# A planned attention and channel-mix kernel: first loads by pair, heads mended in the difference, more work free to go to VectorE, a new order

## The chip, the cores and the metric

One core of one Trainium2 chip runs the whole program. The engines are TensorE (PE, with its weight loads as PEld), VectorE (DVE), ScalarE (ACT), GpSimd (POOL) and SyncE (SP), which here issues every transfer. The metric is the device time of one execution in microseconds; the median of several runs is given, and one execution is taken by the hardware profiler.

## The reference

Blockwise causal attention over q, k and v, each 8 x 8 heads x 576 x 64 in float32, and then an RWKV channel mix on its result (8 x 576 x 512). Cut to what matters:

```python
scores = np.matmul(q, k.transpose(0, 1, 3, 2)) / np.sqrt(D)
mask = (pos[:, None] // 64) >= (pos[None, :] // 64)
attn = softmax(np.where(mask, scores, -1e9))
x = np.matmul(attn, v)                # then heads side by side: b, s, 512
x_prev = x one position earlier       # zeros at the head of each batch
xk = mu_k * x + (1 - mu_k) * x_prev
xr = mu_r * x + (1 - mu_r) * x_prev
k = np.maximum(xk @ w_k, 0)           # 512 -> 1024
out = sigmoid(xr @ w_r) * (k * k @ w_v)
```

## The kernel before

Attention goes by batch (b, 0 to 7), and in a batch by pairs of heads (pr, 0 to 3); a group g is two pairs, and Q is the half of the heads that values are formed for. The channel mix goes by chunks c of positions over all batches: two of 256 positions and eight of 512. Batches are 576 long, so seven batch heads lie inside a chunk.

Every piece of work is a task of a planner (`Plan`) with an engine, a cost, dependencies and the buffers that it takes from rings. TensorE's order is a list written out by name (`TENSOR`). For tasks that more than one engine can do (`flex`), a table (`WHERE`) names the engine. The other engines' queues, and SP's queue of transfers, are laid out by `Plan.order`: tasks are sorted by due time, which is worked back from TensorE's order, and taken when the plan holds them ready. All this runs when the program is built; on the chip each engine works through its own queue in order, with semaphores between them.

Names in TensorE's order, with the profile's lines:

- `q{b}{pr}{n}` (L470): turns the queries (n = 0) or keys (n = 1) of a pair for batches 0 and 1, nine matmuls against an identity. Before it, two loads into `t_ld` (L373) of 288 KB each, one per x, and two casts into `t_nl` (`qk{b}{g}{n}{x}`) must be done, and a copy `ev` out of PSUM follows. One load holds one head of each of the group's two pairs: pair 0 in partitions 0 to 63, pair 1 in 64 to 127.
- For batches 2 to 7 there is no such product: loads, casts into `NB` (L392, L398), a copy of the tail on GpSimd (L516), and then a transposing DMA on SP's queue, `turn` (L534), one for each pair, 24 in all, into `t_qkt`.
- `s{b}{pr}{i}` (L652, L660): scores of a pair, three pieces i, and `s{b}t{Q}` for the last 64 keys. Each piece is followed by an exponential on ScalarE (L679) and, where a piece has a diagonal block, by setting its masked quarter to zero on GpSimd (`zero`, L688).
- `d{b}{Q}`, `e0{Q}` (L725): sums of the exponentials; reciprocal and spreading on VectorE follow (L777, L786). `v{b}{Q}{i}` (L725): values, then their scaling into `t_xt` on VectorE (L833, L835).
- For each chunk and each quarter cc of the 512 channels, `add_mix` forms the difference `t_d` of neighbouring positions (L907, on GpSimd or VectorE), and from it `t_xk` and `t_xr` on VectorE (L920). In a chunk with a batch head inside, GpSimd then writes that column of `t_xk` and `t_xr` anew (`fix`, L935), after the last quarter.
- `k{c}{jc}` (L958): four matmuls of `xk @ w_k`; a relu on ScalarE (L969), and a square (`sq`, L976, L978) on any of three engines. `r{c}{jt}` (L993) and tanh (L1004). `p{c}{jt}` (L1024): eight matmuls of `k*k @ w_v`, the last product on VectorE (L1036), and the store (L1042).
- Until the first `k` task the planner puts idle TensorE time to filling products against the identity (L1062).

Of the kernel before, what the change touches and what calls it, by code (L numbers as in the profile page):

```python
# [24 lines left out]
q000 q001 q011 q010 s000 s010 q031 s001 s011 q020 q021 q030 d00 v000 s012 s030  # L25
q100 q110 s002 s020 s0t0 s021 s032 d01 q101 v010 s0t1 e00 s031 v001 v002 s022
s100 q111 s101 k00 k02 k01 s110 q120 s111 e01 v011 v012 q131 s112 s1t0 q130
k03 s102 q121 k13 k15 k07 k05 k14 k11 k16 d10 s120 s122 k12 k17 r01 k10 s121
v100 v102 v101 s130 s131 r00 r10 r11 s1t1 s132 k04 k06 s200 d11 v111 v110 s201
p11 s202 p00 s210 s212 p01 s2t0 p10 v112 k20 s211 k22 r22 r23 k25 r20 k24 k21  # L30
d20 s230 s231 k26 k27 s232 r21 k23 v200 v201 s2t1 s220 s222 v202 s221 p20 s300
s301 d21 v211 v210 s302 v212 p23 p22 p21 k30 k31 k34 r32 s310 s311 r31 k36 k35
s3t0 s312 r30 k37 s320 s321 d30 k32 k33 s322 s330 v301 v300 v302 s331 s332 r33
s3t1 p31 d31 s400 s402 p33 v312 v311 v310 p30 p32 s401 k40 k41 k42 k43 k47
s410 s411 k46 r40 k45 r43 s4t0 s412 k44 r42 s430 s431 r41 d40 v400 v402 s432
s420 p41 s421 s422 p40 s4t1 v401 d41 s500 s501 p43 v411 v410 s5t0 s510 v412
s512 s502 p42 s511 s530 k50 k51 k57 s532 s520 k56 d50 r53 k53 r50 k52 k55 s531
s5t1 v500 v502 v501 s522 s521 r52 k54 s600 r51 d51 v511 v510 s601 s602 v512
p50 s610 s6t0 p51 p53 s620 s611 p52 s630 s612 k60 k63 s621 s632 k62 k66 k65
r62 k67 s631 k61 d60 s6t1 s622 k64 r60 v600 v602 v601 p60 r63 d61 s700 s702  # L40
p63 r61 v612 v611 v610 s710 s730 p62 s7t0 s731 p61 s712 s7t1 r71 r72 s701 s720
k70 k72 k74 s711 s721 k71 k73 k76 d70 s732 s722 k75 v700 v701 r70 d71 r73 k77
v711 v702 v710 p73 p70 p72 p71 v712 k80 k81 k82 k83 k86 k85 k84 k87 r81 r82
r83 r80 p83 p81 p82 p80 r92 r91 k90 k93 k96 k92 k91 k95 k94 k97 r90 r93 p91
p90 p92 p93b p93a
# [31 lines left out]

class Plan:

    LAT = {"PE": 0.26, "ACT": 0.19, "DVE": 0.16, "POOL": 0.16, "SP": 1.9}
    SWITCH = 0.095
    AHEAD = 25.0
    DMA = 2.0
    BLOCK, FIRST, FETCH = 256, 183, 5.0

    def __init__(self, rings):
# [191 lines left out]
def kernel(  # L281
# [12 lines left out]
    nc = tc.nc  # L294
# [840 lines left out]
```

## Time and profile before

| what | value |
|---|---|
| median of 5 runs | 270.44 us (269.43 to 271.48) |
| the profiled execution | 269.09 us |
| its span | 267.3 us, granted clock 0.994 |
| first product | at 6.86 us |
| DMA, whole span | 51.51 MB, 193 GB/s mean |
| zero blocks on GpSimd (L688) | 128, 208 ns mean |
| relu on ScalarE (L969), 512 columns | 64, 612 ns mean |
| mends on GpSimd (L935) | 7 of `t_xk`, 277 ns mean; 7 of `t_xr`, 409 ns mean |
| turning transfers (L534) | 24, on SP's queue 1.26 to 3.82 us, median 2.10 |

The span runs from the first instruction to the last; what lies between it and the execution's time is before and after it. Busy time of an engine is the union of its instructions; two instructions that follow each other overlap at their ends, so the mean of one times its count is a little more than the busy time. A line such as "A <- B: us, times, longest" says that A's engine stood idle until B ended. The DMA share is the mean of 16 DMA engines, and it can pass 1.0 where packets overlap. A piece of the chain of work is a start, a duration and what ran.

### The profile page before, as it was taken

What the parts mean: (1) busy time and instruction counts of PE and PEld (TensorE: products, weight loads), DVE (VectorE), ACT (ScalarE), POOL (GpSimd) and SP (SyncE); (2) the same over time, 40 slices, a digit from 0 to 9 for tenths busy, and PEclk for the clock granted to TensorE, in tenths of its full rate; (3) what the DMA queues carried; (4) which work ended last, traced back from release to release, by engine and by line L of the source; (5) the groups of instructions that cost most, each with busy time, mean ns of one, the idle gap of its engine ahead of it and who ended that gap; (6) DMA issues with size and microseconds to landing.
All of it is one profiled execution on the core that took longest, in us unless ns stands there. A gap on an engine that the chain in (4) does not pass through costs nothing.

```text
span 267.3 us, 9966 instructions
## 1 busy us (share of the span) xinstructions
PE 248.4 (93%) x4112; PEld 130.3 (49%) x4112; DVE 203.3 (76%) x474; ACT 195.5 (73%) x310; POOL 123.1 (46%) x271
## 2 busy tenths in 40 slices
PE   0999979999999999999989899899999999999995
PEld 0676566554445435544445345444554455444443
DVE  2378998889259976999598988987899099895323
ACT  2699998995999179829966899759758971490750
POOL 3664588537365254633345446354603563270020
PEclk9997999999999999999999999999999999999999
DMA  7999999999989999989979999999995100302104
GB/s 227 317 224 255 255 317 293 275 264 206 223 205 224 201 205 320 184 200 278 207 181 187 183 206 303 172 199 229 296 197 152 42 5 30 129 0 105 55 1 157
DMA packets 118301, 51.51 MB, mean 193 GB/s; under 512 B 102768, under 2 KB 109168, under 8 KB 118256
## 3 DMA queue, kind: packets, MB, share of 16 engines
q1 hardware_dynamic: 118256, 50.88, 82.4%
q8 instruction: 32, 0.52, 0.8%
q14 instruction: 13, 0.11, 0.2%
HBM read 33.56 MB, written 9.44 MB: 161 GB/s over the span
## 4 chain that ended last, share of the span: by engine, by line
PE 56%; ACT 14%; DMA 12%; DVE 7%; issue 5%; SPq 2%; POOL 2%; POOLq 0%; ACTq 0%
PE t_mm L1024 19%; PE t_mm L958 13%; PE t_mm L993 7%; PE t_mm L725 7%; ACT t_e L679 7%; DMA t_ld<-in_q_dram 5%; PE t_s L652 5%; DMA t_qkt<-NB 5%; ACT t_kr L969 3%; SPq L373 2%; DMA t_ld<-in_k_dram 2%; PE t_mm L470 2%; PE t_s L660 2%; ACT NB L392 1%; DVE t_xr L920 1%
## 5 line engine op out<-in xcount | busy, mean ns | idle before, releaser
L679 ACT ACTIVATE t_e<-t_s 128x1024 f16<-128x1024 f32 x96 | 96.1, 1033 | 14.5 <-PE t_s L660 7.4
L958 PE MATMUL t_mm<-t_xk,WK 128*128 128x512 f16 (+1 forms) x320 | 68.7, 358 | 0.8 <-POOL t_xk L935 0.5
L1024 PE MATMUL t_mm<-WV,t_k 128*128 128x512 f16 (+1 forms) x296 | 66.3, 374 | 0.3 <-DVE t_xt L833 0.3
L969 ACT ACTIVATE t_kr<-t_mm 128x512 f32<-128x512 f32 (+1 forms) x80 | 43.0, 569 | 20.5 <-PE t_mm L958 19.3
L688 POOL MEMSET t_e<- 64x128 f16 x128 | 24.4, 208 | 61.8 <-ACT t_e L679 60.0
L958 PEld LDWEIGHTS <-WK 128*128 128x128 f16 x320 | 29.7, 98 | 31.4 <-issue 2.4
L1024 PEld LDWEIGHTS <-t_k 128*128 128x128 f16 x296 | 27.2, 98 | 31.9 <-issue 2.1
L652 PE MATMUL t_s<-t_qkt 64*128 64x256 bf16 (+3 forms) x272 | 35.2, 327 | 3.8 <-ACT t_e L679 2.1
L993 PE MATMUL t_mm<-WR,t_xr 128*128 128x512 f16 x144 | 35.6, 380 | 0.4 <-DVE t_o L1036 0.4
L978 POOL TENSOR_TENSOR t_k<-t_kr 128x512 f16<-128x512 f32 (+1 forms) x26 | 24.0, 931 | 25.7 <-ACT t_kr L969 25.5
L833 DVE TENSOR_TENSOR t_xt<-t_mm,t_rd 128x448 f32<-128x448 f32 (+6 forms) x56 | 30.6, 596 | 6.2 <-PE t_mm L725 5.8
L907 POOL TENSOR_TENSOR t_d<-t_xt 128x512 f32<-128x512 f32 (+1 forms) x24 | 25.5, 1070 | 13.3 <-DVE t_xt L833 12.7
L920 DVE SCALAR_TENSOR_TENSOR t_xr<-t_d,MUR,t_xt 128x512 f16<-128x512 f32 (+1 forms) x40 | 31.5, 811 | 0.0
L1036 DVE SCALAR_TENSOR_TENSOR t_o<-t_t,t_mm 128x512 f32<-128x512 f32 (+1 forms) x37 | 24.0, 664 | 9.3 <-PE t_mm L1024 8.8
L920 DVE SCALAR_TENSOR_TENSOR t_xk<-t_d,MUK,t_xt 128x512 f16<-128x512 f32 (+1 forms) x40 | 29.0, 748 | 1.7 <-POOL t_d L907 1.7
L1004 ACT ACTIVATE t_t<-t_mm 128x512 f32<-128x512 f32 x36 | 21.5, 611 | 11.4 <-PE t_mm L993 11.2
L725 PE MATMUL t_mm<-t_e,VO 128*32 128x64 f16 (+4 forms) x1056 | 27.7, 248 | 1.0 <-issue 1.0
L978 DVE TENSOR_TENSOR t_k<-t_kr 128x512 f16<-128x512 f32 (+1 forms) x29 | 20.1, 710 | 11.0 <-ACT t_kr L969 11.0
L777 DVE RECIPROCAL t_c<-t_mm 128x128 f32<-128x128 f32 (+1 forms) x18 | 15.5, 864 | 16.9 <-PE t_mm L725 16.9
L660 PE MATMUL t_s<-t_qkt 64*128 64x64 bf16 x320 | 23.9, 195 | 1.7 <-ACT t_e L679 1.5
L725 PEld LDWEIGHTS <-VO 128*32 128x32 f16 x1184 | 19.0, 97 | 10.8 <-issue 6.3
L993 PEld LDWEIGHTS <-t_xr 128*128 128x128 f16 x144 | 13.1, 98 | 16.2 <-issue 1.8
(60 smaller groups left out, 270.5 us busy)
## 6 DMA issues: line engine op xcount, KB each, us to landing
out_dram<-t_o SPq DMA_DIRECT2D x35, 256.0 KB, 3.5
t_vl<-in_v_dram SPq DMA_DIRECT2D x32, 256.0 KB, 5.4
t_ld<-in_k_dram SPq DMA_DIRECT2D x48, 128.0 KB, 3.9
t_ld<-in_q_dram SPq DMA_DIRECT2D x24, 256.0 KB, 4.2
t_ld<-in_q_dram SPq DMA_DIRECT2D x8, 288.0 KB, 5.4
t_ld<-in_k_dram SPq DMA_DIRECT2D x8, 288.0 KB, 5.2
t_ld<-in_moe_w_k_dram SPq DMA_DIRECT2D x8, 256.0 KB, 5.5
t_ld<-in_moe_w_v_dram SPq DMA_DIRECT2D x8, 256.0 KB, 4.1
```

Of the source, the lines that this page charges most:

```text
L652: nc.tensor.matmul(PS[:, h, col:col + J * w].rearrange("p (j n) -> p j n", j=J), keys, ask[:, 0:CUT].rearrange("d (p j) -> d j p" if b < T ...
L660: nc.tensor.matmul(PS[:, h, col:col + D], keys, ask[:, CUT:S], start=True, stop=True)
L679: nc.scalar.activation(tiles["e", b, pr][:, :, i, :], tiles["ps", b, pr, i], AF.Exp, scale=ISQ)
L725: nc.tensor.matmul(ps[g * R:g * R + R], lhs, e, start=start, stop=stop, tile_position=(0, g * R))
L833: nc.vector.tensor_tensor(x[:, 0], num[:, 0], r, ALU.mult)
L907: (nc.vector if eng == "DVE" else nc.gpsimd).tensor_tensor(tiles["d", c, cc][:, 0:w], x[:, cc, o + 1:o + w + 1], x[:, cc, o:o + w], ALU.su ...
L920: nc.vector.scalar_tensor_tensor(tiles[name, h][:, cc, o:o + w], tiles["d", c, cc][:, 0:w], (MUK1, MUR1)[n][:, cc:cc + 1], xt_tile(c)[:, c ...
L958: nc.tensor.matmul(ps[:, 0:w], WK[:, cc, jc * P:(jc + 1) * P], tiles["xk", h][:, cc, o:o + w], start=(cc == 0), stop=(cc == CCn - 1))
L969: nc.scalar.activation(tiles["kr", c, jc][:, 0:w], tiles["pk", c, jc][:, 0:w], AF.Relu)
L978: (nc.vector if eng == "DVE" else nc.gpsimd).tensor_tensor(K2, KR, KR, ALU.mult)
L993: nc.tensor.matmul(ps, tiles["xr", h][:, cc, o + jt * P:o + (jt + 1) * P], WR[:, cc], start=(cc == 0), stop=(cc == CCn - 1))
L1024: nc.tensor.matmul(ps[:, 0:w], tiles["k2", h][:, jc, off:off + P], WV[:, jc, cols], start=(jc == 0), stop=(jc == JCn - 1))
```

## The change

Five things change.

1. For the first group of batch 0, each of the four loads is split by pair: eight loads of 64 partitions (144 KB) and eight casts, and a product of pair y waits only for the casts that hold y. All other groups are as before.
2. The batch heads are mended in the difference: after a quarter's `t_d` is formed, one column is copied from `t_xt` over it, on the engine that formed it, so that `t_xk` and `t_xr` come out right by themselves. The two `fix` operations per batch head go; four copies of one column per head come.
3. Zero blocks and relus become `flex`, open to GpSimd or VectorE, and to ScalarE or VectorE. The exponential is written for the used columns alone; all pieces use 512, so its shape stays.
4. The planner's figures for transfers change: a transfer begins 1.2 after its issue, and its lateness is 0.6 in place of 1.9.
5. `TENSOR` and `WHERE` are new. Built with them, VectorE holds 32 relus (24 of 512 columns, 8 of 256) and 53 of the 128 zero blocks; ScalarE keeps 48 relus and GpSimd 75 zero blocks. There are 18 filling tasks where there were 12. SP's queue begins with the two whole key loads of group 1, then the halves.

Of the two tables only some lines are shown.

```diff
-q000 q001 q011 q010 s000 s010 q031 s001 s011 q020 q021 q030 d00 v000 s012 s030
...
-p50 s610 s6t0 p51 p53 s620 s611 p52 s630 s612 k60 k63 s621 s632 k62 k66 k65
...
+q000 q031 q021 q001 q010 s000 s002 q011 s010 q100 s0t0 q110 q020 s011 s001
...
+v511 p52 v510 s602 s630 p51 s610 s6t0 p53 s611 s612 k60 k63 s620 s621 k67 d60
+s632 s622 k64 r60 k61 r61 k66 k62 s6t1 s631 k65 r62 v600 v602 v601 d61 r63
...
-    LAT = {"PE": 0.26, "ACT": 0.19, "DVE": 0.16, "POOL": 0.16, "SP": 1.9}
+    LAT = {"PE": 0.26, "ACT": 0.19, "DVE": 0.16, "POOL": 0.16, "SP": 0.6}
...
-    DMA = 2.0
+    DMA, BEGIN = 1.7, 1.2
...
-        return t["dur"] + t["xfer"] + self.LAT[t["eng"]]
+        begin = self.BEGIN if t["xfer"] else 0.0
+        return t["dur"] + begin + t["xfer"] + self.LAT[t["eng"]]
...
-                        dma = end = max(end, dma) + t["xfer"]
+                        dma = end = max(end + self.BEGIN, dma) + t["xfer"]
...
     tiles = {}
 
 
-    def load(dst_key, make, jobs, dur, xfer, takes=()):
+    def load(dst_key, make, jobs, dur, xfer, takes=(), uses=()):
         def fn():
             if make is not None:
                 tiles[dst_key] = make()
             for dst, src in jobs(tiles[dst_key]):
                 nc.sync.dma_start(dst, src)
-        return plan.add("SP", dur, fn, takes=takes, xfer=xfer)
+        return plan.add("SP", dur, fn, (), takes, uses, xfer=xfer)
 
     on = plan.add
 
...
         for g in range(2):
             for n in range(2):
                 nl = plan.buf("nl")
-                done = []
-                for x in range(2):
-                    ld = plan.buf("ld")
-                    key = ("ld", b, g, n, x)
-                    t = load(key, lambda: new("ld", [P, S], FP),
-                             lambda d, n=n, g=g, x=x: [
-                                 (d, (q, k)[n][b, 4 * g + 2 * x:4 * g + 2 * x + 2]
-                                  .rearrange("y (p j) d -> (y p) (j d)", j=JT))],
-                             0.5, 0.86, takes=[ld])
-
-                    def fn(eng, g=g, n=n, key=key, x=x):
-                        if x == 0:
-                            tiles["nl", b, g, n] = new("nl", [P, JT, P], BF)
-                        convert(eng, tiles["nl", b, g, n][
-                            :, :, x * D:x * D + D],
-                            tiles[key][:, :].rearrange("p (j d) -> p j d", d=D))
-                    done.append(flex(
-                        f"qk{b}{g}{n}{x}", {"POOL": 0.61, "DVE": 0.67,
-                                            "ACT": 0.58},
-                        fn, [t] + done, takes=[] if x else [nl],
-                        uses=[ld] + ([nl] if x else []), lock=("POOL",)))
+                halves = ((0, 1), (1, 2)) if (b, g) == (0, 0) else ((0, 2),)
+                lds = [plan.buf("ld") for _ in range(2)]
+                done = {0: [], 1: []}
+                for lo, hi in halves:
+                    for x in range(2):
+                        key, ld = ("ld", b, g, n, x), lds[x]
+                        rows = slice(lo * D, hi * D)
+                        at = 4 * g + 2 * x
+                        new_ld = [] if lo else [ld]
+                        new_nl = [] if lo or x else [nl]
+                        t = load(key, None if lo else
+                                 lambda: new("ld", [P, S], FP),
+                                 lambda d, n=n, rows=rows, a=at + lo,
+                                 z=at + hi: [
+                                     (d[rows], (q, k)[n][b, a:z].rearrange(
+                                         "y (p j) d -> (y p) (j d)", j=JT))],
+                                 0.5, 0.43 * (hi - lo), new_ld,
+                                 [] if new_ld else [ld])
+
+                        def fn(eng, g=g, n=n, key=key, x=x, rows=rows,
+                               first=bool(new_nl)):
+                            if first:
+                                tiles["nl", b, g, n] = new(
+                                    "nl", [P, JT, P], BF)
+                            convert(eng, tiles["nl", b, g, n][
+                                rows, :, x * D:x * D + D],
+                                tiles[key][rows, :].rearrange(
+                                    "p (j d) -> p j d", d=D))
+                        c = flex(
+                            f"qk{b}{g}{n}{x}" + str(lo) * (hi - lo < 2),
+                            {"POOL": 0.61, "DVE": 0.67, "ACT": 0.58},
+                            fn, [t], new_nl,
+                            [ld] + ([] if new_nl else [nl]), ("POOL",))
+                        for y in range(lo, hi):
+                            done[y].append(c)
                 for y in range(2):
                     m = plan.buf("mm")
                     pr = 2 * g + y
...
                                 tiles["nl", b, g, n][rows, j],
                                 identb[rows, rows], is_transpose=True,
                                 start=(j == 0), stop=(j == JT - 1))
-                    t = on("PE", 0.3, turn, list(done), takes=[m], uses=[nl],
+                    t = on("PE", 0.3, turn, list(done[y]), takes=[m], uses=[nl],
                            name=f"q{b}{pr}{n}", mode="turn", steps=JT)
                     first = not some
 
...
             return
         ebuf = tiles["ebuf", b, pr]
 
+        used = sum(D if a == M else J * (z - a) for _, _, a, z in pieces(b)[i])
+
         def ex():
-            nc.scalar.activation(tiles["e", b, pr][:, :, i, :],
-                                 tiles["ps", b, pr, i], AF.Exp, scale=ISQ)
-        t = on("ACT", 0.905, ex, [pe] + ([ready["x", b, pr, 0]] if i else []),
+            nc.scalar.activation(tiles["e", b, pr][:, :, i, 0:used],
+                                 tiles["ps", b, pr, i][:, :, 0:used], AF.Exp,
+                                 scale=ISQ)
+        t = on("ACT", 0.175 + 0.73 * used / 512, ex, [pe] + ([ready["x", b, pr, 0]] if i else []),
                uses=[sbuf, ebuf])
         ready["x", b, pr, i] = t
 
-        def zero():
+        def zero(eng):
             for col, kc, a, z in pieces(b)[i]:
                 if a == kc * 32 and a < M:
-                    nc.gpsimd.memset(
+                    (nc.vector if eng == "DVE" else nc.gpsimd).memset(
                         tiles["e", b, pr][D:P, :, i, col:col + J * (
                             z - a)].rearrange(
                             "p h (j n) -> p h j n", j=J)[:, :, :, 0:D // J],
                         0.0)
         n = sum(a == kc * 32 and a < M for col, kc, a, z in pieces(b)[i])
         if n:
-            ready["z", b, pr, i] = on("POOL", 0.15 * n, zero, [t], uses=[ebuf])
+            ready["z", b, pr, i] = flex(
+                f"z{b}{pr}{i}", {"POOL": 0.19 * n, "DVE": 0.09 * n}, zero, [t],
+                uses=[ebuf], lock=())
 
     def probs(b, head, kc, a, z):
 
...
             mixed[c, 0], mixed[c, 1] = [], []
         f = W[c] / CH
         w = W[c]
-        alts = {"DVE": 0.06 + 0.59 * f, "POOL": 0.06 + 0.96 * f}
+        heads = [b * S - CHUNKS[c][0] for b in range(B)
+                 if 0 < b * S - CHUNKS[c][0] < w]
+        alts = {"DVE": 0.06 + 0.59 * f + 0.07 * len(heads),
+                "POOL": 0.06 + 0.96 * f + 0.22 * len(heads)}
         usual = "DVE" if cc % 2 else "POOL"
 
         def fn(eng):
-            tiles["d", c, cc] = new("d", [P, CH], FP)
+            d = tiles["d", c, cc] = new("d", [P, CH], FP)
             x = xt_tile(c)
-            (nc.vector if eng == "DVE" else nc.gpsimd).tensor_tensor(
-                tiles["d", c, cc][:, 0:w], x[:, cc, o + 1:o + w + 1],
-                x[:, cc, o:o + w], ALU.subtract)
+            e = nc.vector if eng == "DVE" else nc.gpsimd
+            e.tensor_tensor(d[:, 0:w], x[:, cc, o + 1:o + w + 1],
+                            x[:, cc, o:o + w], ALU.subtract)
+            for at in heads:
+                e.tensor_copy(d[:, at:at + 1], x[:, cc, o + at + 1:o + at + 2])
         sub = flex(f"d{c}{cc}", {usual: alts[usual], **alts}, fn,
                    list(xt_of[c][cc]), takes=[d], uses=[xtbuf[h]])
         for n in range(2):
...
                 "DVE", 0.14 + 0.525 * f, mul, [sub] + mu_ready,
                 takes=[buf] if first else [],
                 uses=[d, xtbuf[h]] + ([] if first else [buf]), lock=BOTH))
-            if cc < CCn - 1:
-                continue
-
-            for b in range(B):
-                at = b * S - CHUNKS[c][0]
-                if 0 < at < w:
-                    def fix(n=n, at=at, name=name):
-                        nc.gpsimd.tensor_tensor(
-                            tiles[name, h][:, :, at:at + 1],
-                            xt_tile(c)[:, :, at + 1:at + 2],
-                            (MUK, MUR)[n][:, :].unsqueeze(2), ALU.mult)
-                    mixed[c, n].append(on(
-                        "POOL", 0.16, fix, list(mixed[c, n]),
-                        uses=[buf, xtbuf[h]], lock=BOTH))
 
     act = {}
 
...
                uses=[tiles["xkb", h]] + ([] if first else [k2b]),
                name=f"k{c}{jc}", mode="full", steps=4)
 
-        def relu():
+        def relu(eng):
             tiles["kr", c, jc] = new("kr", [P, CH], FP)
-            nc.scalar.activation(tiles["kr", c, jc][:, 0:w],
-                                 tiles["pk", c, jc][:, 0:w], AF.Relu)
-        t = on("ACT", 0.06 + 0.43 * f, relu, [t], takes=[kr], uses=[m])
+            dst, src = tiles["kr", c, jc][:, 0:w], tiles["pk", c, jc][:, 0:w]
+            if eng == "ACT":
+                nc.scalar.activation(dst, src, AF.Relu)
+            else:
+                nc.vector.tensor_scalar_max(dst, src, 0.0)
+        t = flex(f"re{c}{jc}", {"ACT": 0.06 + 0.43 * f, "DVE": 0.07 + 0.54 * f},
+                 relu, [t], takes=[kr], uses=[m], lock=())
 
         def sq(eng):
             KR, K2 = tiles["kr", c, jc][:, 0:w], tiles["k2", h][:, jc, o:o + w]
```

## The prediction

> **What bounds the kernel now.** I read the page's busy line first, then the table by stages of 20 us, then the chain of work that ended last, SP's queue in order of time and its waits, and the rows by shape for prices.
>
> ```profile
> PE 248.4 (93%) x4112; PEld 130.3 (49%) x4112; DVE 203.3 (76%) x474; ACT 195.5 (73%) x310; POOL 123.1 (46%) x271
> ```
>
> ```profile
> 20.00:40.00 20.00, 17.16 (x509) 12.31 (x509) 18.60 (x59) 19.62 (x34) 11.85 (x27) 0.91 1.05 276
> ...
> 80.00:100.00 20.00, 18.69 (x298) 9.12 (x299) 18.69 (x41) 12.60 (x19) 9.39 (x21) 1.00 0.95 212
> ...
> 120.00:140.00 20.00, 19.03 (x262) 8.93 (x257) 16.01 (x35) 17.25 (x27) 8.04 (x20) 1.00 0.98 219
> ...
> 160.00:180.00 20.00, 18.92 (x344) 9.58 (x342) 18.27 (x37) 15.27 (x24) 10.57 (x23) 1.00 1.08 226
> 180.00:200.00 20.00, 20.00 (x416) 10.32 (x415) 16.57 (x42) 15.81 (x26) 8.37 (x22) 1.00 1.11 242
> 200.00:220.00 20.00, 20.00 (x328) 9.48 (x325) 13.15 (x30) 16.88 (x26) 10.30 (x22) 1.00 0.32 70
> ```
>
> The columns after the stage's length are busy time of PE, PEld, DVE, ACT and POOL, then the granted clock, the DMA share and GB/s. TensorE is at 93%, but the column to read is the share of the DMA engines: about 1.0 in every stage up to 200 us, then 0.32. The transfers are a second full resource for three quarters of the run, and TensorE is without a gap only from 180 on. The chain says which of the two sets the end:
>
> ```profile
> 165.51 6.51 DMA t_qkt<-NB
> 172.02 0.05 issue
> 172.06 0.39 PE t_s L652 x2
> ...
> 229.56 7.01 PE t_mm L958 x32
> 236.58 3.45 PE t_mm L993 x16
> 240.03 6.91 PE t_mm L1024 x32
> ...
> 264.26 0.42 DVE t_o L1036
> ```
>
> The 18th of the 24 turning transfers (batch 6, pair 1) is issued at 165.51 and lands at 172.02; score s610 starts at once, and TensorE then works to 264.26. So the end is a landing plus 92.2 us of matmuls ordered behind it. SP's queue and its waits show how that transfer comes so late:
>
> ```profile
> 146.64 3.82 SPq L534 DMA_TRANSPOSE t_qkt<-NB  x1
> ...
> 165.51 6.64 SPq L534 DMA_TRANSPOSE t_qkt<-NB  x3
> 172.20 5.55 SPq L373 DMA_DIRECT2D t_vl<-in_v_dram  x5
> ```
>
> ```profile
> SPq L534 <- POOL t_e L688: 11.8, 7, 3.3
> ...
> SPq L534 <- POOL t_xk L935: 2.2, 2, 1.2
> ```
>
> SP issues one transfer behind the other and hardly rests, except at the turns: the shortest of the 24 takes 1.26 us, the median 2.10. They wait for GpSimd's casts and tail copies, which stand in GpSimd's queue behind its zero blocks (L688) and mends (L935).
>
> **Part 1, halves.** Four 288 KB loads become eight of 144 KB, and four casts become eight of half the partitions. The built order decides what that brings: SP now issues the two whole key loads of group 1 first, then the halves. The first product waited for three loads, 864 KB (6.86 us); now it waits for 2 x 288 + 2 x 144 = 864 KB and one issue more (0.42). So the start gains nothing: 0 to +0.4 us. A cast's row is 667 to 750 ns on 128 partitions; I take the same for 64, so 4 x 0.7 = 2.8 us more, spread over ACT, DVE and POOL, which between 0 and 10 us are busy 2.98, 3.82 and 4.40 us only. On the queue, eight issues at 0.45 are 3.6 us for 1,152 KB, while the bytes at the 266 GB/s of the first 10 us need 4.3: the issues hide behind the bytes. A half tile could move as fast as a whole one (cost 0), or only at half the rate (+4.3); no half-height load with such rows is in the trace. The 64-partition tails (128 KB) land after 4.7 to 4.9 us against 5.4 for 256 KB, nearer to the first than twice the time would be; I take 0 and keep +4.3 for the range.
>
> The trace gives whole tiles 317 GB/s in the page's second slice. [...]
>
> **Part 2, mends.** 14 POOL operations (277 and 409 ns mean) go; 28 one-column copies come, 19 on POOL and 9 on DVE. Bounds per copy: a memset of one column (0.10) and the mend (0.41) on POOL; a 4-column memset (0.06) and the edge copy (0.36) on DVE. With 0.28 and 0.1: POOL -4.8 + 5.3 = +0.5, DVE +0.9. TensorE waited 0.5 us in all for a mend; on its path -0.5 to +0.4, taken as 0. But a mend waited on POOL for DVE's last mix (7.9 and 4.3 us in all) with casts queued behind it; the new copy follows a subtraction of its own engine.
>
> **Part 3, relu and zero blocks.** By the built order 24 relus of 512 columns and 8 of 256 move from ACT to DVE, and 53 of 128 zero blocks from POOL to DVE.
>
> ```profile
> L969 ACT ACTIVATE t_kr<-t_mm 128x512 f32<-128x512 f32 x64 | 37.4, 612 | 19.9 <-PE t_mm L958 19.3 <-POOL VO L398 0.3
> ...
> L688 POOL MEMSET t_e<- 64x128 f16 x128 | 24.4, 208 | 61.8 <-ACT t_e L679 60.0
> ...
> L1036 DVE SCALAR_TENSOR_TENSOR t_o<-t_t,t_mm 128x512 f32<-128x512 f32 x35 | 23.2, 678 | 8.7 <-PE t_mm L1024 8.2 <-issue 0.4
> ```
>
> A relu on DVE is not in the trace: 0.43 (a cast of 512) to 0.76 (the copy from PSUM); nearest is L1036, one pass from PSUM, 0.68, and 0.42 for 256. A DVE zero block writes 64 words: between 0.06 (4 columns) and 0.27 (256 words), by proportion 0.11. DVE gets 24 x 0.68 + 8 x 0.42 + 53 x 0.11 = 25.5; other moved work (7 casts to t_nb and 5 squares fewer, 5 half squares, 3 subtractions, 5 casts and evictions more) nets about -0.5; with the mends DVE goes to 203 + 26 = 229 us, 86% of the span. ACT loses 24 x 0.58 + 8 x 0.35 = 16.7 and takes back 2.6: 181. POOL loses 53 x 0.19 = 10.1, net about 110. All three lie beside TensorE and the transfers; if DVE's cover is gone, see the slower rival. A DVE relu now stands behind a mix (0.87) in DVE's queue, and the k chain behind it waits for one of four PSUM buffers.
>
> **Part 4, the order.** Bytes are the same, so I count what stands ahead of the transfer that sets the end. Ahead of the 18th turn: the same loads, stores and turns, plus one v load of 256 KB, 1.25 us (five took 5.55, one of them half). It is now pair 3. Behind s630 in the new TensorE order stands exactly what stood behind s610 (32 k, 16 r, 4 d, 12 v, 25 scores) but one p fewer, 1.73 us (6.91 / 4). Net +1.25 - 1.73 = **-0.5**. The later turns have little to spare: the 22nd and 23rd have two v loads more ahead (+2.5) and, for the 23rd, one p and three scores less behind, about 2.6.
>
> **What the freer GpSimd queue gives.** Of SP's 29.1 us of waits at turns, 16.0 end at zero blocks or mends. Much of that the queue covers; visible is the share below 1: 0.05 and 0.02 of 20 us, in 80-100 and 120-140, **1.4 us**. If the full share is that of 20-60 (1.085), the stages from 60 to 140 (1.01, 0.95, 1.05, 0.98) lack 7.0. Bounds 0 and 7.0; I take 1.4, since five more casts to t_nb go onto POOL.
>
> **Sum.** 0 + 0 + 0 - 0.5 - 1.4 = -1.9. The profiled execution took 269.09 (span 267.3 and 1.8 around it) and would take 267.2. The median of the runs is 270.44, 1.35 higher, so 268.5.
>
> **Rivals.** (a) The turns wait as before, as other POOL work ends them: only the order counts, -0.5, 269.9, within 0.5% (1.35 us, about what a measurement of this kernel tells from no change). For it: the casts moved to POOL; against: 16.0 of 29.1 us. (b) Slower: VectorE becomes the bound between 20 and 180 us. It has 135.2 us of work there in 160; 8 half and 12 whole relus, some 45 zero blocks and the mends add 17.2, so 152.4. Its fullest stages there (18.60, 18.69, 18.27 of 20) run at 92.6%: 152.4 / 0.926 = 164.6, +4.6, less the 1.9: 273.1. It decides once VectorE needs more than 92.6% of that stretch. Against: ends overlap in busy time, 40 to 80 us is slack (28.8 of 40), and the transfers, not VectorE, set 172. (c) Halves at half rate: +4.3 - 1.9, 272.8.
>
> **How the numbers follow.** Forecast 0.45, (a) 0.27, (b) 0.20, (c) 0.08. Faster 0.45, same 0.27, slower 0.28. Low end: -0.5 with the middle of 1.4 and 7.0, -4.7, 265.7. High end: up to 272.8, leaving (b)'s full price out. The forecast's own range is 265.7 to 269.1.
>
> **What would show it.** Right: turns with a median below 2.1 us, batch 6's landing followed by gapless TensorE, DMA share at or above 1.0 in 80-140, first product at 6.9. Wrong: gaps of TensorE that end at DVE t_kr or t_xk, DVE above 93% in several stages, or first loads that land later than 6.4 us.

## The result and the profile after

| | before | after |
|---|---|---|
| median of all runs | 270.01 us (267.03 to 273.15, 47 runs) | 273.52 us (270.88 to 276.64, 28 runs) |
| ratio | | 1.013, 95% interval 1.0107 to 1.0153 |
| profiled execution, its span | 269.09, 267.3 us | 275.55, 273.6 us |
| first product, first score | 6.86, 9.87 us | 7.62, 11.71 us |
| first `k` task | 28.80 us | 36.31 us |
| first turn issued | 45.22 us | 53.05 us |
| last landing that the chain waits for | 172.02 us, 18th turn | 206.41 us, 22nd turn |
| end of TensorE's work | 264.26 us | 270.33 us |

The changed kernel is 1.3% slower, 3.5 us of 270. The profiled execution of after is a slow one, 2 us above the median of its runs, so a single stage of it counts below only where other runs show the same. The granted clock is no reason for the difference: its mean is 0.991 over the 28 runs of after and 0.989 over the 81 runs of before that went with the experiments.

The page's busy line of after and its groups by shape (busy us, mean ns, idle before):

```profile
PE 251.3 (92%) x4124; PEld 128.9 (47%) x4124; DVE 226.8 (83%) x569; ACT 185.9 (68%) x282; POOL 110.4 (40%) x222
```

```profile
L998 DVE TENSOR_SCALAR t_kr<-t_mm 128x512 f32<-128x512 f32 x24 | 16.4, 687 | 5.5 <-PE t_mm L983 5.1
...
L948 POOL COPY t_d<-t_xt 128x1 f32<-128x1 f32 x19 | 7.4, 390 | 1.2
L720 DVE MEMSET t_e<- 64x64 uint32 x53 | 5.1, 112 | 3.0 <-ACT t_e L710 0.9
```

The loads of the three engines came out as counted (forecast 229, 181 and 110), and so did a relu (0.68) and a zero block (0.11) on VectorE. The one-column copy on GpSimd is dearer, 0.39 for 0.28.

The table by stages of 20 us, columns as in the prediction (PE, PEld, DVE, ACT, POOL, clock, DMA share, GB/s):

```profile
20.00:40.00 20.00, 16.81 (x479) 11.16 (x479) 17.82 (x60) 14.46 (x21) 7.76 (x20) 0.91 0.87 224
40.00:60.00 20.00, 17.50 (x359) 9.63 (x350) 16.89 (x53) 18.28 (x31) 11.63 (x25) 1.00 1.00 261
...
80.00:100.00 20.00, 19.18 (x332) 9.25 (x329) 17.75 (x51) 14.43 (x21) 10.10 (x18) 1.00 1.12 219
...
120.00:140.00 20.00, 19.99 (x242) 8.96 (x230) 18.93 (x46) 16.07 (x24) 9.34 (x19) 1.00 1.17 215
...
180.00:200.00 20.00, 20.00 (x362) 9.92 (x362) 18.09 (x41) 16.03 (x25) 10.37 (x24) 1.00 1.24 242
200.00:220.00 20.00, 19.17 (x301) 9.07 (x294) 18.14 (x50) 15.73 (x23) 8.66 (x18) 1.00 0.63 132
```

From 60 to 180 us TensorE is busier than before, 117.1 of 120 us against 114.9, and the share of the transfers is above 1.0 in 80 to 140, as forecast. What is lost lies ahead: in 20 to 40 the share falls from 1.05 to 0.87, 276 GB/s to 224, and ScalarE's busy time from 19.62 to 14.46. SP's queue shows what the transfers lack there:

```profile
11.77 5.76 SPq L388 DMA_DIRECT2D t_ld<-in_q_dram  x2
...
23.17 0.62 SPq L1080 DMA_DIRECT2D MUK<-in_moe_mu_k_dram  x1
...
24.40 2.82 SPq L388 DMA_DIRECT2D t_ld<-in_moe_w_k_dram  x4
```

The wait in it, and the same loads before:

```profile
SPq L388 <- POOL t_nl L413: 4.2, 1, 4.2
```

```profile
12.93 1.04 SPq L1051 DMA_DIRECT2D MUK<-in_moe_mu_k_dram  x1
...
15.50 3.61 SPq L373 DMA_DIRECT2D t_ld<-in_moe_w_k_dram  x4
```

Two loads take 5.76 us on the queue: SP stands until a load buffer comes free. The new order has the load of mu and the key weights behind that stall, at 23.17 and 24.40; before they went out at 12.93 and 15.50. No `k` can start without them, but they are not what the first `k` waits for in the end: the fourth cast of these weights ends at 33.2 us and the fourth `t_xk` at 33.3, and the first `k` starts at 36.31, without a wait, behind fillings and scores of TensorE's own list (its rows stand under "The mends").

The chain that ended last (start, duration, what):

```profile
173.05 5.90 DMA t_qkt<-NB
178.99 0.39 PE t_s L681 x2
...
188.91 0.97 PE t_mm L983 x4
189.88 0.86 PE t_mm L1022 x4
190.75 0.86 PE t_mm L983 x4
...
198.37 0.57 POOL t_d L945
198.94 7.47 DMA t_qkt<-NB
206.46 0.39 PE t_s L681 x2
...
263.39 6.94 PE t_mm L1053 x40
270.35 0.42 DVE t_o L1065
```

Two landings bind in place of one. The 18th turn lands at 178.95, 6.9 us later than before, and from the start of its score to the end it is 91.3 us instead of 92.2. Of the 91.3, 0.8 is TensorE's wait for the second landing, so the work is 90.5, 1.7 less than before. The lines at 188.91 and 190.75 are the same four matmuls; the first follows scores, the second another product of the same kind, and it is 0.11 us shorter. The waits of SP's queue at turns did not shrink:

```profile
SPq L563 <- POOL t_e L720: 12.2, 8, 2.4
SPq L563 <- POOL NB L413: 7.2, 3, 2.7
SPq L563 <- POOL t_d L945: 6.3, 3, 2.6
```

All waits at turns come to 35.8 us (29.1 before), those at zero blocks to 12.2 (11.8); those at the old mends, 4.2 before, are gone.

### The profile page after: what moved, and what is told of

Same layout as the page of the kernel before. It is cut to its first block, busy times and chain, and to the rows that moved or that the text cites. A ratio compares the mean times of both kernels' runs of the same rounds, so it can differ in the third digit from the quotient of the medians.

```text
span 273.6 us, 9972 instructions
## 1 busy us (share of the span) xinstructions
PE 251.3 (92%) x4124; PEld 128.9 (47%) x4124; DVE 226.8 (83%) x569; ACT 185.9 (68%) x282; POOL 110.4 (40%) x222
## 5 line engine op out<-in xcount | busy, mean ns | idle before, releaser
L983 PE MATMUL t_mm<-t_xk,WK 128*128 128x512 f16 (+1 forms) x320 | 69.8, 361 | 0.1
L983 PEld LDWEIGHTS <-WK 128*128 128x128 f16 x320 | 28.9, 99 | 30.9 <-issue 3.8
L681 PE MATMUL t_s<-t_qkt 64*128 64x256 bf16 (+3 forms) x272 | 35.8, 327 | 4.0 <-DMA t_qkt<-NB 2.7
L1007 POOL TENSOR_TENSOR t_k<-t_kr 128x512 f16<-128x512 f32 (+1 forms) x23 | 21.8, 949 | 37.2 <-ACT t_kr L996 19.8
L996 ACT ACTIVATE t_kr<-t_mm 128x512 f32<-128x512 f32 (+1 forms) x48 | 26.6, 572 | 13.8 <-PE t_mm L983 12.7
L720 POOL MEMSET t_e<- 64x128 f16 x75 | 14.3, 206 | 49.0 <-ACT t_e L710 47.4
L959 DVE SCALAR_TENSOR_TENSOR t_xk<-t_d,MUK,t_xt 128x512 f16<-128x512 f32 (+1 forms) x40 | 30.6, 786 | 0.2
L945 POOL TENSOR_TENSOR t_d<-t_xt 128x512 f32<-128x512 f32 (+1 forms) x21 | 22.1, 1051 | 15.5 <-DVE t_xt L867 14.5
L959 DVE SCALAR_TENSOR_TENSOR t_xr<-t_d,MUR,t_xt 128x512 f16<-128x512 f32 (+1 forms) x40 | 27.8, 721 | 0.1
L998 DVE TENSOR_SCALAR t_kr<-t_mm 128x512 f32<-128x512 f32 (+1 forms) x32 | 19.6, 620 | 6.7 <-PE t_mm L983 6.3
L681 PEld LDWEIGHTS <-t_qkt 64*128 64x128 bf16 x272 | 12.5, 97 | 17.9 <-issue 10.6
L689 PEld LDWEIGHTS <-t_qkt 64*128 64x128 bf16 x320 | 14.0, 97 | 13.5 <-issue 12.2
```

Source lines behind the costliest of these rows:

```text
L681: nc.tensor.matmul(PS[:, h, col:col + J * w].rearrange("p (j n) -> p j n", j=J), keys, ask[:, 0:CUT].rearrange("d (p j) -> d j p" if b < T ...
L689: nc.tensor.matmul(PS[:, h, col:col + D], keys, ask[:, CUT:S], start=True, stop=True)
L945: e.tensor_tensor(d[:, 0:w], x[:, cc, o + 1:o + w + 1], x[:, cc, o:o + w], ALU.subtract)
L959: nc.vector.scalar_tensor_tensor(tiles[name, h][:, cc, o:o + w], tiles["d", c, cc][:, 0:w], (MUK1, MUR1)[n][:, cc:cc + 1], xt_tile(c)[:, c ...
L983: nc.tensor.matmul(ps[:, 0:w], WK[:, cc, jc * P:(jc + 1) * P], tiles["xk", h][:, cc, o:o + w], start=(cc == 0), stop=(cc == CCn - 1))
L996: nc.scalar.activation(dst, src, AF.Relu)
```

## The experiments

### One part at a time, planned anew

Four kernels take one part out of after, or put one into before, and leave the rest to the planner, which lays out all queues again. a: after with whole first loads. b: before with the halves. c: after with every relu on ScalarE and every zero block on GpSimd. d: after's code with before's two tables.

```diff
a: -                halves = ((0, 1), (1, 2)) if (b, g) == (0, 0) else ((0, 2),)
a: +                halves = ((0, 2),)
c: +ENGINE.update({k: 'ACT' if k[:2] == 're' else 'POOL' for k in ENGINE if k[:2] == 're' or (k[0] == 'z' and k[1:].isdigit())})
```

> The changed kernel with part 1 undone: the first group of batch 0 is loaded and cast whole, four loads of 288 KB; everything else, the new order too, is kept. Theory H (the half loads start the kernel late, and the fixed order carries the lateness through): first score within 0.5 us of the 9.9 us of before, DMA rate between 5 and 10 us back above 300 GB/s, first turning transfer issued before 49 us (53.1 in the changed kernel), and the time at or below the kernel before, ratio 0.99 to 1.002. Theory O (the new order and the new table of engines are the cost by themselves): first score early as well, but the stalls between 15 and 50 us stay, and the ratio stays at 1.008 to 1.015.

> The kernel before with part 1 alone: the first group in halves, old order, mends, relus and zero blocks as before; the halves stand first on SP's queue. Theory H: DMA between 5 and 10 us near 236 GB/s in place of 344, loads behind the halves land 1 to 2 us later, ratio 1.004 to 1.012. Theory O: the halves only move the first product forward (to under 6.3 us) and cost nothing, ratio 0.995 to 1.003.

> The changed kernel with part 3 undone: all relus on ScalarE, all zero blocks on GpSimd; halves, mends and TensorE's new order are kept. Theory V (VectorE, at 227 us of work, is the bound): VectorE busy near 203 us and a ratio to before of 1.00 or less. Theories H and O: the early lateness stays, ratio 1.01 or more, and more than that if the order needs ScalarE's freed time.

> The changed kernel's code (halves, mends in the difference, planner figures) with the old order and the old table of engines, so relus on ScalarE and zero blocks on GpSimd. Against the halves alone it adds the mends and the planner's figures. Theory H: as the halves alone, within 0.4% of it. Theory O: ratio to before 0.995 to 1.003, since the old order is back. If the mends are a gain by themselves it is 0.3 to 1% faster than the halves alone.

Measured: a 285.54 us (no ratio is formed), b 281.76, 1.036 (1.028 to 1.044); c 282.20, 1.039 (1.031 to 1.048); d 280.77, 1.034 (1.026 to 1.042). All are far slower than both kernels, whichever part moved and in whichever direction. So these runs price the planner's new queues, not the part: order and table were made for one program. From here on the planner's order is written down and replayed, and only the named thing differs:

```diff
-    for t in plan.order(TENSOR.split()):
+    for n in FROZEN.split():
+        t = plan.fills.pop() if n == "-1" else plan.tasks[int(n)]
         t["fn"]()
```

### The halves

e is before with each of its first four loads issued as two transfers of 64 partitions, casts whole. f is after with the whole 288 KB in the first half's place and no second transfer. k is after with the halves ahead of the two key loads of group 1, and with pairs 0 and 1 turned and scored first. The eight half casts stay in f, and e has none of them: no run takes them out alone.

```diff
e: -   (d, (q, k)[n][b, 4 * g + 2 * x:4 * g + 2 * x + 2] ...)
e: +   (d[lo * D:hi * D], (q, k)[n][b, 4 * g + 2 * x + lo:4 * g + 2 * x + hi] ...)
e: +   for lo, hi in (((0, 1), (1, 2)) if (b, g) == (0, 0) else ((0, 2),))
f: -   lambda d, ...: [(d[rows], (q, k)[n][b, a:z] ...)]
f: +   lambda d, ...: [] if lo else [(d, (q, k)[n][b, a:a + 2] ...)]
```

> The kernel before with every engine's order kept as it was, and one thing changed: each of the first group's four loads is issued as two half-height transfers, one after the other; casts stay whole. It adds four issues and no bytes. Theory H (half-height transfers are slow, and a late start is carried to the end): first product 0.5 to 1.5 us later than 6.9, DMA rate between 5 and 10 us below 300 GB/s, ratio to before 1.003 to 1.01. Theory N (the transfers' shape costs nothing; what was lost came from new queues): first product within 0.4 us, ratio 0.997 to 1.003.

> The changed kernel with every engine's order kept as it is, and one thing changed: the first half of each load carries the whole 288 KB and the second half is not issued, so four issues fewer, and the eight half casts wait for whole transfers. Theory H: first score before 11 us (11.7 in the changed kernel), first turning transfer 1 us or more earlier, ratio to before 1.005 or less. Theory N: the first score moves by under 0.5 us and the ratio stays at 1.010 to 1.016.

> After with one thing moved: the first pair's halves (q, k of pair 0, then of pair 1) are issued ahead of the two whole key loads of group 1, and TensorE turns and scores pairs 0 and 1 first; from about 20 us on every queue is as in after. Theory S (the late first score, 11.71 against 9.87, is carried to the end): first score near 8 us, ratio to before 0.997 to 1.006, about 3 us under after. Theory T (the start is absorbed: k00 waits for the mu and key weight loads, which SP issues at 23 to 27 us behind its stall for a load buffer): first score near 8, k00 still at 35 to 37 us, ratio 1.010 to 1.015.

Measured: e 271.56, 1.0088 (1.0053 to 1.0123); f 272.21, 1.0121 (1.0072 to 1.0170); k 276.02, 1.0198 (1.0150 to 1.0245). The first 10 us by stages of 5 us (last two columns DMA share and GB/s), before, e, after and f:

```profile
0.00:5.00 5.00, 0.00 (x0) 0.00 (x0) 1.96 (x8) 1.95 (x2) 1.50 (x9) 1.00 0.63 189
5.00:10.00 5.00, 3.14 (x46) 2.57 (x48) 1.86 (x3) 1.03 (x2) 2.90 (x5) 1.00 1.05 344
```

```profile
0.00:5.00 5.00, 0.00 (x0) 0.00 (x0) 1.96 (x8) 0.00 (x0) 1.50 (x9) 1.00 0.46 126
5.00:10.00 5.00, 1.83 (x28) 1.48 (x28) 0.76 (x1) 2.62 (x3) 1.58 (x3) 1.00 0.90 261
```

```profile
5.00:10.00 5.00, 1.52 (x29) 1.26 (x30) 0.75 (x1) 2.46 (x5) 1.57 (x3) 1.00 1.01 236
```

```profile
5.00:10.00 5.00, 1.52 (x29) 1.26 (x30) 1.50 (x2) 1.83 (x3) 2.23 (x4) 1.00 1.00 363
```

The stage from 5 to 10 us moves less where it has half-height loads: 233 to 285 GB/s in b, c, d, e, n, after, i and k, at shares of 0.90 to 1.01, and 326 to 375 in a, before, f, h, j, l, m, o and p, which have none, at 0.97 to 1.07. At about the same share less is brought. By 10 us e has moved (126 + 261) x 5 us = 1.94 MB where before has 2.67; the missing 0.73 MB are 2.1 us at 344 GB/s, and e costs 0.88% of 270, 2.4 us. In the old order the price is shown, and the ranges of Theory H hold. In the new one, after and f differ by 0.1%, while i and j below, the same pair with the mends put back, differ by 0.9%; there it lies between.

k scores for the first time at 8.0 us, 3.7 sooner than after, and is no faster (its ratio lies above the ranges of both its theories): its first `k` is still at 34.1. So the late first score is not what reaches the end. p below says the same with whole loads.

### The mends

h is before with the mends in the difference; i is after with the two GpSimd operations back behind the last mix.

```diff
h: +            for at in heads:
h: +                e.tensor_copy(d[:, at:at + 1], x[:, cc, o + at + 1:o + at + 2])
h: -                        nc.gpsimd.tensor_tensor(tiles[name, h][:, :, at:at + 1], ...)
i: the same lines, the other way round
```

> The kernel before with every engine's order kept and the mends alone changed: 28 one-column copies behind the subtractions, 14 products on GpSimd gone. My prediction priced them at nothing on the path: ratio 0.997 to 1.003. If GpSimd's waits for the last mix held casts and turning transfers back, a gain: 0.99 to 0.997. If the copies on GpSimd (0.39 us each in the changed kernel) stand in the way: 1.003 to 1.01.

> After with every queue kept in its order, only the mends of the batch heads put back: the one-column copies into the difference go (19 on GpSimd, 390 ns, 9 on VectorE, 153 ns), and one four-column product on GpSimd per tile (409 and 277 ns, 14 of them) stands behind the last mix. Theory A (the mends cost in the new order what they cost alone in the old one, 1.1% in h): ratio to before 1.002 to 1.008, 270.5 to 272. Theory B (a queue that was laid out for copies loses what the mends would give; the mends' place is worth nothing by itself): 1.010 to 1.018, as after. Lag of TensorE at s400 tells them apart: under A at least 2 us less than after.

Measured: h 272.21, 1.0113 (1.0055 to 1.0171); i 274.56, 1.0191 (1.0143 to 1.0238). The mends cost in the old order and, by the two pairs of the new one (after against i, f against j: -0.6% and +0.2%), nothing that can be told from none. That is Theory B of i, a little above its range. Why h is slower its profile can't say: its first copy runs at 53.8 us, and by the first turn, with the same work as before, that execution was already 2.7 us late (47.89 against 45.22). The same holds for after and i, which do the same work until 58.6 us. TensorE's way to the first `k` in the two (start, busy us, line; in square brackets the idle time before, and "issue" where the profile shows nothing that ended it):

```profile
32.01 0.84 PE L759 MATMUL t_mm<-t_e,VO 128*32 128x256 f16 x28 [2.48 <-issue]
...
34.58 1.25 PE L1091 MATMUL t_mm<-identb 128*128 128x128 bf16 x10
...
36.31 1.03 PE L983 MATMUL t_mm<-t_xk,WK 128*128 128x256 f16 x4
```

```profile
29.05 1.47 PE L840 MATMUL t_mm<-t_e,VO 128*32 128x256 f16 x28 [0.46 <-issue]
...
34.02 1.48 PE L1071 MATMUL t_mm<-t_xk,WK 128*128 128x256 f16 x12
```

One work, 2.3 us apart, and 2.0 of it is one standstill of TensorE in the middle of a values product. after, f, g and i have it at values products of this shape, 0.46 us (i) to 3.3 us (f) long; h has one of 2.58 us at 35.82, where before has 0.96. What ends it the profile doesn't show. Single executions of this kernel scatter so much in their first 50 us.

### Relus and zero blocks

g is after with all of them on ScalarE and GpSimd; l is before with after's 32 relus and 53 zero blocks on VectorE; o is before with the zero blocks there alone.

```diff
g: +ENGINE.update({k: 'ACT' if k[:2] == 're' else 'POOL' for k in ENGINE if k[:2] == 're' or (k[0] == 'z' and k[1:].isdigit())})
l: -            nc.scalar.activation(tiles["kr", c, jc][:, 0:w], ..., AF.Relu)
l: +            if f"re{c}{jc}" in ON_DVE: nc.vector.tensor_scalar_max(dst, src, 0.0)
l, o: -         nc.gpsimd.memset(
l, o: +         (nc.vector if f"z{b}{pr}{i}" in ON_DVE else nc.gpsimd).memset(
```

> The changed kernel with every engine's order kept as it is in the sequence of tasks, and only the relus put back on ScalarE and the zero blocks on GpSimd, each at its own place in the sequence. Theory V (VectorE's load is the cost): faster than the changed kernel, ratio to before below 1.008, VectorE busy near 203 us. Theory S (the move to VectorE relieves ScalarE and is worth having in this order): slower than the changed kernel, ratio 1.02 or more, with ScalarE busy near 200 us.

> Before with every queue kept and the 32 relus and 36 zero-block tasks that after has on VectorE put there, nothing else. Theory G (GpSimd's and ScalarE's freer queues help, as g suggests with 0.6%): ratio 0.992 to 0.998, the turns' waits at zero blocks below 11.8 us. Theory V (VectorE becomes the bound): 1.010 to 1.025, gaps of TensorE that end at t_kr or t_xk on VectorE. Neither if 0.998 to 1.010.

> Before with every queue kept and only the 36 zero-block tasks on VectorE (53 blocks), the relus left on ScalarE. Tells which half of part 3 costs the 1.6% of l. If the relus (0.69 us each, behind mixes in VectorE's queue): ratio 0.994 to 1.003, and the turns' waits at zero blocks under 11.8 us. If the zero blocks (a short block now stands in VectorE's queue and waits for ScalarE's exp): 1.008 to 1.016.

Measured: g 273.71, 1.0188 (1.0131 to 1.0244); l 274.30, 1.0156 (1.0118 to 1.0195); o 272.58, 1.0060 (1.0023 to 1.0098). TensorE's waits from 84 to 126 us (us in total, times, longest), in l, in before and in after:

```profile
PE t_mm L1116 <- DVE t_rd L869: 1.7, 1, 1.7
PE t_mm L1116 <- DVE t_o L1128: 1.7, 1, 1.7
PE t_mm L814 <- DVE t_rd L869: 0.7, 1, 0.7
PE t_mm L1116 <- DVE t_xt L922: 0.6, 1, 0.6
```

```profile
PE t_mm L993 <- DVE t_o L1036: 0.4, 1, 0.4
PE t_mm L1024 <- DVE t_xt L833: 0.3, 1, 0.3
PE t_mm L958 <- DVE t_xt L833: 0.2, 1, 0.2
```

```profile
PE t_s L681 <- DMA t_qkt<-NB: 0.5, 2, 0.3
PE t_s L689 <- ACT t_e L710: 0.2, 1, 0.2
```

In l TensorE waits 4.7 us for VectorE there, in before 0.9, in after not at all; n below, which has the same load in the old order, waits 4.3 us at the same places, and o 2.4. l's loss is 1.56% of 270, 4.2 us. So VectorE does become the bound with this move, in the old order (Theory V of l, though the waits end at reciprocals, a scaling and a last product, not at `t_kr`: VectorE works ahead of them without a gap of 0.1 us, from 85 to 92 and from 117 to 122 us, and what is late is whatever stands last in its queue); in the new order the same load hides: after against g gives -0.6%, j against m below +0.4%, which is nothing that can be told from none. By o, which falls between the ranges that were set for it, 0.60 of the 1.56% are the zero blocks. Where g has them back on GpSimd, SP's waits at zero blocks are 16.9 us against after's 12.2: the move does shorten these waits, and the time gains nothing that the intervals of g and after keep apart (g lies between the ranges of its two theories).

### The order

j is f with the mends back: the order and the moved engines are left. m is j with the engines back: the new order alone, but for the eight half casts, which f, j, m and p keep (0.66 to 0.75 us each in f, like a whole one). p is m with k's start. n is before's order with e, h and l together.

> After with every queue kept, the first loads whole (as in f) and the mends back (as in i): of the change only the new order and the moved relus and zero blocks are left. If halves and mends carry the loss by themselves (0.9% and 1.1% alone in the old order) and the new order gains what I forecast, ratio 0.990 to 1.000. If the new order itself is later at its start (the two whole key loads ahead, the mu and key weight loads behind the stall of SP's queue), 1.008 to 1.015, as f.

> After with every queue kept, and three parts of the change undone at once: first loads whole (f), mends back (i), relus on ScalarE and zero blocks on GpSimd (g). Only the new order is left. In the runs so far the first turn is issued 2.8 us earlier than after's without the halves, 2.1 without the mends, 4.6 without both, 2.9 without the moved engines. Theory C (the loss is the lateness of the first turn, carried through a stream of transfers that is full from there on, and the parts add up in it): first turn at 45 to 47 us, span 267 to 269, ratio 0.996 to 1.006. Theory O (the new order is slow by itself): first turn about 48.5 as in j, ratio 1.008 to 1.015.

> Before with every queue kept and all parts but the new order: the first four loads in two half-height transfers each (e), mends in the difference (h), relus and zero blocks on VectorE (l). By Theory C the lateness of the first turn adds up, 2.9 + 2.7 + 2.0: issued at 51 to 53 us, ratio at least 1.020 to 1.036 (the sum of the three alone is 3.6%). If the three hide behind one another, first turn 48 to 50 and ratio 1.010 to 1.018; the new order is then worth nothing.

> m with the start of k: the loads of pairs 0 and 1 whole and ahead of the two key loads of group 1, TensorE scores pairs 0 and 1 first. First score at 9 to 10 us. Theory C: the time follows the first turn and not the first score, so within 0.4% of m although the score starts 2 us earlier. If the first score matters by itself: 1.5 to 2 us under m, ratio 0.990 to 0.998.

| | median us | ratio, 95% interval | first `k` us | first turn us |
|---|---|---|---|---|
| j, order and engines | 272.26 | 1.0103 (1.0062 to 1.0144) | 34.5 | 48.46 |
| m, order and half casts | 272.57 | 1.0065 (1.0025 to 1.0105) | 34.4 | 48.67 |
| p, m with pairs 0 and 1 first | 273.08 | 1.0112 (1.0077 to 1.0147) | 35.0 | 49.25 |
| n, all but order and half casts | 278.73 | 1.0299 (1.0250 to 1.0347) | 30.9 | 48.14 |

The new order with the half casts is slower, by 0.65%, 1.8 us. All other parts in the old order cost 3.0% (the sum of e, h and l alone is 3.6). With both, after is at 1.3%: the order takes back 1.7 points of what the parts cost without it. Theory C, that lateness of the first turn adds up part by part, falls: m's ratio lies between the ranges of C and O, m's first turn is no earlier than j's, n's at 48.14 instead of 51 to 53, and the differences of the first turn that suggested it are of the size of the scatter above.

Where the order loses the time can be read, why only in part. The first 60 us of before, m and after (columns as in the tables above; PE's busy time comes first), and the filling products of before and after, all of which lie in that stretch:

```profile
0.00:60.00 60.00, 49.35 (x1118) 32.79 (x1119) 44.51 (x130) 50.70 (x84) 34.76 (x84) 0.97 1.03 269
```

```profile
0.00:60.00 60.00, 47.23 (x1096) 30.63 (x1100) 45.64 (x134) 50.18 (x83) 29.35 (x77) 0.97 0.98 255
```

```profile
0.00:60.00 60.00, 44.73 (x1005) 28.48 (x1008) 44.33 (x132) 45.05 (x68) 26.64 (x66) 0.97 0.91 240
```

```profile
L1062 PE MATMUL t_mm<-identb 128*128 128x128 bf16 x24 | 3.9, 285 | 0.0
```

```profile
L1091 PE MATMUL t_mm<-identb 128*128 128x128 bf16 x36 | 5.3, 293 | 0.0
```

Without fillings (5.1 in m) TensorE has done 45.5 us of work in before by then, 42.1 in m and 39.4 in after. Over all profiles it is 44.0 to 45.8 in the seven kernels with the old order and 39.4 to 42.9 in the eight with the new one, so the loss lies there: the two ranges don't overlap. From 60 to 180 us m does 2.4 us more than before. Beside m's 3.4 us stand three terms: a first product that is 0.9 later (7.76 us), 1.2 more of fillings, and idle time in values products that is 1.5 longer (2.5 against 1.0) and scatters. In the seven kernels with the old start the first `k` lies at 28.8 to 31.5 us, in the new order without half loads (f, j, m, p) at 34.4 to 36.5. In m, as in after, its operands are ready some 3 us sooner. That the loads of mu and the key weights behind SP's stall cost time by themselves is not shown: no run has them ahead of it in the new order.

The new order also goes over more often between `k`, `r` and `p` and other products, 125 times against 109, counted in the two lists. Between 181 and 262 us of after, four matmuls of `k` take 0.86 to 0.88 us (start to next start) ahead of `k` or `r` and 0.96 to 0.97 ahead of scores or values; in before 0.87 and 0.95 to 0.97. At 0.10 us a change, the way back taken at the same price, 16 would be 1.6 us, an estimate. The busy time does not show it: m's TensorE is busy longer by 1.5 than before's 248.4, both at a mean clock of 0.994, and 1.2 of that are the twelve more fillings.

```profile
PE 249.9 (93%) x4124; PEld 129.0 (48%) x4124; DVE 201.0 (75%) x475; ACT 197.3 (73%) x314; POOL 115.2 (43%) x270
```

### The landing that the chain named

q is before with four stores, two loads (three transfers) and both transfers of a tail load moved on SP's queue from ahead of the 18th turn to behind the 20th.

> Before with every queue kept, only SP's moved: four stores of t_o (128 KB each), two loads (q or k of batch 7) and the q half of batch 7's tail load, which stand ahead of the 18th turn, go behind the 20th. If the end is a landing of that turn plus the matmuls behind it, as I forecast, the turn is issued about 5 us earlier, but TensorE, which lost 1.0 us waiting for it (start minus work done 23.1 at s600, 24.1 at s610), can give back at most that: 0.994 to 0.999. If SP then waits for the turn's casts with the moved transfers behind it, or the later turns slip, 1.000 to 1.010.

Measured: 271.84 us, 1.000 (0.996 to 1.004). SP's queue and the chain of q:

```profile
161.29 5.86 SPq L615 DMA_TRANSPOSE t_qkt<-NB  x3
```

```profile
173.03 3.82 DMA t_ld<-in_q_dram
176.87 0.62 ACT NB L473
...
178.47 0.39 PE t_s L733 x2
```

The turn goes out 4.2 us sooner, and nothing is gained: TensorE now waits 1.7 us at s620, and the chain leads to one of the loads that were moved. Had the end been that landing plus the work behind it, 4.2 us would have been 1.6%, which the interval excludes; the 1.0 us that TensorE waited for the landing before, the most that could be won, lies at its edge. With the transfers full (shares of 1.08 and 1.11 from 160 to 200 us of before), the landing that the chain names is here one of several that are about equally late. In m, too, the 18th turn goes out at 165.6 us, as before, and the kernel is slower. q also shows that replaying a written-down order costs nothing clear of noise.

No kernel of the study is faster than before.

## Why the prediction was wrong

It forecast 268.5 (range 265.7 to 272.8); the median is 273.52, outside it and on the other side. Its sum was 0 + 0 + 0 - 0.5 - 1.4. The step that failed is the path: it took the 18th turn's landing for what sets the end and priced the order by what stands ahead of and behind it. The loss arose in the first 60 us instead, and q shows that this landing didn't set the end.

- **Part 1, halves, taken as 0: mis-sized.** Measured alone 2.4 us, in the new order between 0.1% and 0.9%. The term rested on whole bytes "at the 266 GB/s of the first 10 us"; stages with the halves show 233 to 285, those with whole loads 326 to 375. The measured price alone lies about midway between the bounds 0 and +4.3 (4.4 at that rate, as these KB are 1024 bytes). What the prediction named as its own refutation, first loads that come late, is what is seen: the cast that the first product waits for starts at 6.90 us, behind its load, and the limit was 6.4. That a cast of 64 partitions takes as long as one of 128 held (0.66 to 0.75 us in after, both).
- **Part 2, mends, taken as 0: held**, in the new order (-0.6% and +0.2% in the two pairs). In the old order they cost 1.1%; the cause isn't shown.
- **Part 3, relus and zero blocks, hidden: held**, loads and prices to a few per cent. The cover is the new order: without it the price is 1.6%. VectorE is above 93% in four stages of after (98.9% from 60 to 80 us), which the prediction named as a sign against it, but TensorE is without a gap in that stage.
- **Part 4, order, -0.5: wrong**, measured +1.8 (0.7 to 2.8), the half casts included. Of its two terms the one behind the landing held: -1.73 forecast, 90.5 us of work against 92.2 measured, and from the 22nd turn's landing at 206.41 to 270.33 TensorE has no gap. The one ahead, +1.25, was +6.9 in after, where the first turn is already 7.8 us late. The step looked at one place and not at the first 60 us, where TensorE does 3.4 us less of its work in m and 6.1 less in after. And moving that landing is worth nothing in itself (q). What in the new start costs the time is narrowed down, not shown.
- **The freer GpSimd queue, -1.4: did not come.** Waits at zero blocks fell only against g and m (16.9 and 15.7 us), not against before (11.8); and those at casts into `NB` and at subtractions grew from 2.1 and 4.1 to 7.2 and 6.3.
- **Rivals.** (b), 273.1, is the nearest number to the result, and that is luck: its mechanism is shown in l and n, but not in after, where it was priced, and VectorE runs beyond its limit of 92.6% there without holding TensorE up. (c), 272.8, had part of the right cause.
- **Signs of being right.** Only the share of the transfers came. The turns' median on SP's queue is 2.28 us, not below 2.1, and the first product comes at 7.62, not 6.9.

Together: order with half casts 0.65% and half loads 0.1 to 0.9%, mends and engines none, make 0.8 to 1.6% against 1.3 measured; each term has an interval of some 0.4 to 0.6 points either way.

## What to carry to other kernels

Where a list of tasks fixes the order, read its first stage as closely as its last: how much work the bounding engine has done by then, how much filling the list holds, and which loads stand behind a wait for a buffer. Price a landing that the chain names by what the engine waits for it, here 1.0 us before the change; put 4.2 us ahead in q, it gained nothing (ratio 0.996 to 1.004). A part undone alone is only priced if every queue is held, and even then its price belongs to that order: the same move cost 1.6% in one and nothing in the other. A single profile of this kernel can't settle less than 2 to 3 us of its start; pairs of medians can.

## What the runs showed of the hardware

- The stage from 5 to 10 us moves 233 to 285 GB/s where it has 144 KB loads into 64 partitions (b, c, d, e, n, after, i, k), at a DMA share of 0.90 to 1.01, and 326 to 375 where it has none (a, before, f, h, j, l, m, o, p), at 0.97 to 1.07.
- Four matmuls of `k`, 512 columns each, take 0.96 to 0.97 us ahead of scores or values and 0.86 to 0.88 ahead of `k` or `r` between 181 and 262 us of after; in before 0.95 to 0.97 and 0.87.
- A cast of 576 columns takes 0.66 to 0.75 us on 64 partitions as on 128 (after: ScalarE 0.67, GpSimd 0.66 to 0.67, VectorE 0.74 to 0.75).
- A one-column copy on GpSimd takes 189 ns in the median of after and up to 1372 (mean 390), 526 in the median of h (mean 411); on VectorE 153 to 155, without spread.
- TensorE stood still in the middle of a values product for 0.46 us in i, 0.9 in g, 0.96 in before, 2.48 in after, 2.58 in h and 3.3 in f, and the profile shows nothing that ended it.
